# Chunk-wise products of w from a product tree through DRAM, in a fused RWKV-7 and gated-FFN kernel

## The chip, the cores and the metric

The kernel runs on one core of a Trainium2 chip. The number that counts is the device time of one execution in microseconds. The kernel before has a median of 846.03 us over 8 runs (844.63 to 849.34). A single execution was taken apart by the hardware profiler; that one took 847.05 us.

In what follows PE is TensorE's matmul side and PEld its weight load, DVE is VectorE, ACT is ScalarE, POOL is GpSimd and SP is SyncE, which here only issues DMAs.

## The reference

Two blocks, one behind the other. The first is a recurrence over 768 time steps with a 40 x 40 state for each of 4 batches and 8 heads, the second a feed-forward block on 3072 tokens of 320 features:

```python
B, H, S, D = r.shape                      # 4, 8, 768, 40
for t in range(S):
    y[:, :, t] = einsum('bhd,bhde->bhe', r_t, state)
    Sa = einsum('bhde,bhe->bhd', state, a_t)
    state = state * w_t[:, :, None, :] - einsum('bhd,bhe->bhde', Sa, b_t)
    state = state + einsum('bhd,bhe->bhde', v_t, k_t)
x = y.transpose(0, 2, 1, 3).reshape(3072, 320)
h = x @ w_in                              # w_in 320 x 2048, w_out 2048 x 320
out = (h * cos(h)) @ w_out
```

w lies between 0.85 and 0.95. w_in and w_out come as 64-bit floats, which the kernel turns into 32-bit ones in its first part, from the raw words.

## The kernel before

**Chunks.** The recurrence runs in 24 chunks of C = 32 steps. Inside a chunk it is done with matrices, and for that every chunk needs W, the running product of w over its steps: a is multiplied by W one step earlier (`wx`, whose first entry is 1), b and k are divided by W (multiplied by the reciprocal `rw`), and the state is multiplied by W of the last step (`wc`) at the chunk's end. In natural layout a tile has batch and time on the partitions, 4 x 32, and heads and features along the row. Transposed it has two heads' features on the partitions and, per pair of heads, batch and time along the row.

**p1, the first preparation, by pairs of chunks.** `p1_w` (L330) transposes w of two chunks on PE into one PSUM pair (`wT`). ACT copies the first time step into `w1`, DVE clears that step in PSUM, and a `tensor_tensor_scan` per chunk (L340) gives the running products in `wb`. POOL copies the last step out as `wc`. `p1_a` (L345), once for each chunk, transposes `wb` back on PE into `wn`, transposes a beside it, and then DVE takes the reciprocal of `wn` (`rw`, L361) and multiplies a's transpose by `wx` into `aT` (L363); POOL sets the first entry of `wx` to 1 (L357) and makes b times `rw` (`bn`, L366). `p1_b` transposes `bn`, `p1_n` multiplies aT by bT. For each four chunks DVE then inverts 32 x 32 triangular matrices for all of them at once: `inverse`, 31 steps of two instructions (L414, L418) between two transposes (L406, L422), whose result `rt` is needed by `ch_s` of the first of the four.

**p2 and main, by chunk.** `p2_v`, `p2_k` and `p2_g` make the transposes of v, r and k and the Gram matrices; `ch_t`, `ch_q`, `ch_x`, `ch_s` and `ch_z` carry the state `qz` through the chunk and write `yt`, which goes through DRAM (`xd`) and comes back as `xT`.

**The second part.** The feed-forward block is cut into pieces (`first_a`, `first_b` and two `second` for each of 12 groups of tokens and 4 column blocks). Pieces of tokens that are ready fill the gaps of the recurrence; those that are left run at the end, from about 665 us on without any p1.

**The order** is written out by hand. For each chunk the list `segs` names t, v, q, k, x, g, s, z, the p1 segments pw, pa, pa1, pb, pn of a later pair, and M, a place for a piece. The loop issues them in turn; `fill` says how many steps of the inverse and of the weights' conversion go in after each. If the list comes to s while `rt` is missing, pieces are issued, each with four inverse steps, until it is there. `later(n, work)` issues work, mostly DMAs, n steps on. The p1 of a pair lies one to four chunks ahead of its use: pairs 4 and 6 in chunk 3, pair 8 in chunk 4, 10 in 5, 12 in 7, 14 in 9, 16 in 11, 18 in 13, 20 in 15, 22 in 17. Chunk 4 begins at 182 us in the profile, chunk 5 at 228, chunk 7 at 293, chunk 11 at about 418 and chunk 15 at about 542.

**PSUM.** `at` gives PSUM pairs in turn from a ring of two. A new user waits until the last reader of the user before last is through.

**DMA queues.** SP issues nearly all loads in order, four DMAs of 40 KB for each tensor and chunk, in pieces of 160 bytes. At the start ACT issues a of chunks 0 and 1, POOL a of chunks 2 and 3.

**Filler.** `busy` and `shifted` issue matmuls on zeros (`idle`) whose result nobody uses: `shifted` one-column ones, 56 in chunk 2 and 48 in chunk 19.

Of the kernel before, what the change touches and what calls it, by code (L numbers as in the profile page):

```python
# [12 lines left out]
ALU = mybir.AluOpType  # L13
# [7 lines left out]
def kernel(  # L21
# [124 lines left out]
    def load(c, names, via=nc.sync):  # L146
        for n in names:
            for i in range(B):
                via.dma_start(
                    nat[n, c][blk[i], :, :D],  # L150
                    src[n][i, :, c * C : (c + 1) * C, :].rearrange("h t d -> t h d"),
                )

    for c in range(2):
        load(c, "w")
        load(c, "a", nc.scalar)
    for n, c in (("b", 0), ("b", 1), ("w", 2), ("w", 3), ("b", 2), ("b", 3)):
        load(c, n)
    load(0, "kvr")

# [8 lines left out]
    load(2, "a", nc.gpsimd)  # L169
    load(3, "a", nc.gpsimd)  # L170
# [4 lines left out]
    w1 = kept("w1", [P, 4 * B, C], 2, 0.0, on=nc.vector)  # L175
    bn_b = kept("bn", [P, H, DP], 7, 0.0, padding, nc.vector)
    kn_b = kept("kn", [P, H, DP], 2, 0.0, padding, nc.vector)
# [7 lines left out]
    idle = const.tile([P, 512], BF16, tag="idle", name="idle")  # L185
# [144 lines left out]
    def p1_w(c):  # L330
        ps = at("wT")
        for i in range(2):
            turned(ps[:, i], nat["w", c + i])

        for i in range(2):
            nc.scalar.copy(w1[i][:, :, 0:1], b4(ps[:, i])[:, :, 0:1])
        nc.vector.memset(ps[:, :, ::C], 0.0)
        for i in range(2):
            wb = ring.tile([P, 4 * P + 1], F32, tag="wb", name="wb")
            nc.vector.tensor_tensor_scan(wb[:, 1:], ps[:, i], flat(w1[i]), 0.0, ALU.mult, ALU.add)  # L340
            wc = ring.tile([P, 4 * B], F32, tag="wc", name="wc")
            nc.gpsimd.tensor_copy(wc, wb[:, C::C])
            G["wb", c + i], G["wc", c + i] = wb, wc

    def p1_a(c):  # L345
        if c < 4:
            wn = ps_h.tile([P, 512], F32, tag="h", name="wn")
            aps = ps_o.tile([P, 512], F32, tag="o", name="aps")
        else:
            ps = at("wn")  # L350
            wn, aps = ps[:, 0], ps[:, 1]
        for j in range(4):
            nc.tensor.transpose(
                wn[:, j * P : (j + 1) * P], G["wb", c][:, j * P + 1 : (j + 1) * P + 1], ident
            )

        nc.gpsimd.memset(G["wb", c][:, : 4 * P : C], 1.0)  # L357
        G["wx", c] = b4(G["wb", c][:, : 4 * P])
        turned(aps, nat["a", c])
        rw = ring.tile([P, H, D], F32, tag="rw", name="rw")  # L360
        nc.vector.reciprocal(rw, unpad(wn.rearrange("p (h d) -> p h d", h=H)))  # L361
        aT = ring.tile([P, 4, P], F32, tag="aT", name="aT")
        nc.vector.tensor_tensor(  # L363
            aT.rearrange("p j (b t) -> p (j b) t", b=B), b4(aps), G["wx", c], ALU.mult
        )
        nc.gpsimd.tensor_tensor(unpad(bn_b[c % 7]), unpad(nat["b", c]), rw, ALU.mult)  # L366
        G["rw", c], G["aT", c] = rw, aT
# [207 lines left out]
    def ch_z(c):  # L575
# [3 lines left out]
        for bb in range(B):  # L579
            for e in range(2):  # L580
                mm(
                    ps[bb // 2][full[e], bb % 2, : 4 * N72], idle[blk[bb], :DP],
                    idle[blk[bb], : 4 * N72], True,
                )
# [147 lines left out]
    def p1(c):  # L732


        def first_w():
            p1_w(c)
            if c == 4:
                for i in range(2):
                    later(1, lambda i=i: load(6 + i, "w"))

        def an_a(i):
            p1_a(c + i)
            if c == 4:
                later(1, lambda: load(6 + i, "ab"))
            elif i and c >= 2 and c + 3 < NCH:
                for m in range(6):
                    later(
                        9 + m // 3 if c == 2 else 2 + m, lambda m=m: load(c + 2 + m % 2, "wab"[m // 2])
                    )

        return [first_w, lambda: an_a(0), lambda: an_a(1), lambda: p1_b(c), lambda: p1_n(c)]
# [17 lines left out]
    with tc.manual_schedule():  # L769
# [24 lines left out]
        def busy(n, after=False):  # L794


            ps = ps_h.tile([P, 512], F32, tag="h", name="busy")
            if after:
                nc.vector.memset(tick, 1.0)
                nc.tensor.matmul(  # L800
                    ps[:1, :], lhsT=tick, rhs=idle, start=True, stop=True, skip_group_check=True
                )
            for _ in range(n):
                mm(ps, idle[:, :P], idle, True)
# [8 lines left out]

        first, other = p1(0), p1(2)
        for seg in (*first[:3], *other[:3], *first[3:], *other[3:]):
            step(seg)
        p2_in(0)
# [4 lines left out]
        for n, seg in ((12, v), (0, k), (0, g), (6, main(0)[2]), (6, None), (4, v1), (0, k1), (0, g1)):  # L822
            for _ in range(n):
                inv_steps.pop(0)()
            if seg:
                step(seg)
            else:
                for m in range(3):
                    w_work[m][0]()
                p2_in(1)  # L830
                p2_kn(1)
        while inv_steps:
            inv_steps.pop(0)()
            if 2 < len(inv_steps) < 9:
                busy(1, True)
# [16 lines left out]
        N_PAD = {2: 56, 19: 48}  # L852
        M = object()
        for c in range(NCH):
# [10 lines left out]
            elif c == 3:  # L865
                pw4, pa4, pa5, pb4, pn4 = p1(4)
                pw, pa, pa1, pb, pn = p1(6)
                segs = [
                    t, pw4, M, q, pa4, M, x, pa5, M, s, pw, M, pb4, pa, M, pn4, pa1, M, z, M, pb, v,
                    pn, k, M, g,  # L870
                ]
                fill = (2, 3)
            elif c == 4:
                pw, pa, pa1, *p8 = p1(8)
                segs = [t, v, M, q, M, k, x, M, g, M, s, M, z, M, pw, M, pa, pa1, M]
                fill = (2, 0)
            elif c == 5:
                pw, pa, pa1 = p1(10)[:3]
                pb, pn = p8
                segs = [t, M, pb, q, M, pn, v, M, x, k, M, s, pw, M, g, M, z, M, pa, pa1, M]  # L880
            elif c % 4 == 0 and q0 < NCH:
                pb, pn = p1(q0)[3:]
                segs = [t, v, M, q, M, k, x, M, g, M, s, pb, M, z, M, pn, M, M]
            elif c % 4 == 1 and q0 < NCH:
                pw, pa, pa1 = p1(q0 + 2)[:3]
                segs = [t, M, pw, q, M, x, k, M, s, v, M, z, M, pa, M, g, M, pa1, M]
            elif c % 4 == 2 and q0 < NCH:
                pb, pn = p1(q0 + 2)[3:]
                segs = [t, M, pb, q, M, pn, v, M, x, M, s, k, M, g, M, z, M, M]
            elif c % 4 == 3 and q0 + 4 < NCH:  # L890
                fill = (2 if c == 7 else 1, 0)
                pw, pa, pa1 = p1(q0 + 4)[:3]
                segs = [t, M, pw, q, M, x, k, M, s, v, M, z, M, pa, M, g, M, pa1, M]
            else:
                segs = [t, v, M, q, M, x, k, M, g, M, s, M, M, z, M, M]
# [8 lines left out]
            if c in (2, 19):  # L904
# [59 lines left out]
```

## Time and profile before

| | |
|---|---|
| median of 8 runs | 846.03 us (844.63 to 849.34) |
| the profiled execution | 847.05 us, of it 845.0 us span |
| PE busy | 751.0 us, 89% |
| DVE busy | 511.5 us, 61% |
| ACT busy | 377.0 us, 45% |
| POOL busy | 197.2 us, 23% |
| scans of w (L340) | 24, mean 1212 ns |
| reciprocals (L361) | 24, mean 2150 ns |
| transposes wn (L353) | 96, 273 ns median |

The page cuts the span into 40 slices of 21 us and gives each engine's busy share in tenths, and beside it the clock that PE was granted. A view by windows gives busy microseconds in stretches of choice. The list of waits says which engine stood idle until whose instruction ended; the timeline lists instructions with start and duration. PE's matmuls overlap, so the distance between starts says more of their cost than the duration of one.

### The profile page before, as it was taken

How to read it: one execution, taken by the hardware profiler on the slowest of the kernel's cores; microseconds unless marked ns; L12 is line 12 of the kernel's file. 1: busy time of each engine (PE TensorE's matmuls, PEld its weight loads, DVE VectorE, ACT ScalarE, POOL GpSimd, SP SyncE). 2: the span in 40 equal slices, each digit the busy share in tenths (PEclk: the TensorE clock that was granted, in tenths of full speed). 3: DMA queues.
4: the chain of work that ended last, by engine and by line, in shares of the span. 5: the costliest groups of instructions: out<-in, count | busy, mean ns of one | idle time of the engine just before them, and what ended most of it. 6: DMA issues, size and time to landing. Idle time of an engine off the chain costs nothing.

```text
span 845.0 us, 37607 instructions
## 1 busy us (share of the span) xinstructions
PE 751.0 (89%) x16830; PEld 576.5 (68%) x16830; DVE 511.5 (61%) x1076; ACT 377.0 (45%) x707; POOL 197.2 (23%) x343
## 2 busy tenths in 40 slices
PE   4447777996898979999998999998999999999997
PEld 3424456774676757787776777776777777777775
DVE  8688868779534796335796345796355784323331
ACT  1216676353153433546344436435445443554343
POOL 4405634230303203212221221230221222011000
PEclk9758889998899999999998999999999999999999
DMA  7556453331133312313214114224211211101000
GB/s 98 108 86 184 126 149 85 63 68 35 39 54 57 60 36 53 64 36 68 55 37 82 44 26 70 54 40 71 54 26 36 46 33 43 36 20 35 19 16 16
DMA packets 181856, 49.10 MB, mean 58 GB/s; under 512 B 156992, under 2 KB 178496, under 8 KB 181696
## 3 DMA queue, kind: packets, MB, share of 16 engines
q1 hardware_dynamic: 179264, 46.05, 27.0%
q8 instruction: 132, 2.16, 1.0%
q10 hardware_dynamic: 2176, 0.33, 0.3%
q0 software_dynamic: 256, 0.33, 0.2%
q14 instruction: 28, 0.23, 0.1%
HBM read 38.80 MB, written 7.86 MB: 55 GB/s over the span
## 4 chain that ended last, share of the span: by engine, by line
PE 64%; DVE 23%; ACT 7%; issue 3%; DMA 2%; POOL 0%; SPq 0%; ACTq 0%; DVEq 0%
PE ph L101 23%; PE po L101 19%; DVE inv_tmp L414 5%; DVE inv L418 5%; PE dps L101 3%; PE x0ps L101 3%; PE gram L101 2%; PE vT L298 2%; PE sps L101 2%; PE nps L101 2%; DVE rw L361 2%; DVE turns L678 2%; DVE wb L340 1%; PE qps L101 1%; DVE gT L686 1%
## 5 line engine op out<-in xcount | busy, mean ns | idle before, releaser
L101 PE MATMUL po<-w_out_sb,gT 128*128 128x320 f32 x768 | 225.3, 440 | 0.0
L101 PE MATMUL ph<-xT,w_in_sb 128*128 128x256 f32 x768 | 192.2, 397 | 4.9 <-DVE gT L686 3.7
L101 PEld LDWEIGHTS po<-w_out_sb,gT 128*128 128x128 f32 x768 | 140.4, 191 | 53.9 <-issue 2.6
L101 PEld LDWEIGHTS ph<-xT,w_in_sb 128*128 128x128 f32 x768 | 144.6, 197 | 34.2 <-issue 13.4
L676 ACT ACTIVATE turns<-ph,rnd 128x512 f32<-128x512 f32 x96 | 63.8, 686 | 161.7 <-PE ph L101 161.4
L678 DVE SCALAR_TENSOR_TENSOR turns<-turns,ph 128x512 f32<-128x512 f32 x96 | 63.7, 683 | 113.2 <-ACT turns L676 113.1
L603 POOL TENSOR_TENSOR qz<-qz,wc 128x160 f32<-128x160 f32 x92 | 42.7, 482 | 257.2 <-DVE qz L602 256.5
L686 DVE TENSOR_TENSOR gT<-ph,turns 128x512 f32<-128x512 f32 x96 | 65.8, 686 | 36.8 <-ACT turns L683 36.8
L414 DVE TENSOR_TENSOR inv_tmp<-u,inv 128x31 f32<-128x31 f32 (+15 forms) x186 | 71.0, 382 | 4.4
L418 DVE TENSOR_TENSOR inv<-inv,inv_tmp 128x31 f32<-128x31 f32 (+15 forms) x186 | 69.1, 372 | 6.4
L683 ACT ACTIVATE turns<-turns,half_pi 128x512 f32<-128x512 f32 x96 | 69.3, 722 | 3.1
L682 ACT ACTIVATE turns<-turns 128x512 f32<-128x512 f32 x96 | 60.2, 627 | 21.6 <-DVE turns L678 21.6
L361 DVE RECIPROCAL rw<-wn 128x320 f32<-128x320 f32 x24 | 51.6, 2150 | 7.9 <-PE wn L298 7.7
L101 PE MATMUL ph<-xT,w_in_tail 64*128 64x256 f32 x384 | 55.1, 405 | 0.0
L602 DVE TENSOR_TENSOR qz<-dps,qz 128x160 f32<-128x160 f32 x92 | 28.9, 315 | 33.0 <-PE dps L101 32.9
L508 ACT COPY s<-sT 128x512 f32<-128x512 f32 x46 | 24.6, 586 | 51.6 <-PE sT L504 51.6
L101 PEld LDWEIGHTS ph<-xT,w_in_tail 64*128 64x128 f32 x384 | 33.6, 189 | 10.7 <-issue 7.1
L614 POOL TENSOR_TENSOR yt<-yt,wb 128x512 f32<-128x512 f32 x24 | 31.3, 1302 | 22.4 <-DVE yt L609 22.4
L436 POOL COPY vp<-nat_v 128x320 f32<-128x320 f32 x25 | 12.0, 481 | 95.5 <-DMA nat_v<-in_v_dram 66.2
L101 PE MATMUL sps<-x,rt 32*32 32x72 f32 x1536 | 22.6, 242 | 13.1 <-DVE rt L422 10.9
L101 PEld LDWEIGHTS sps<-x,rt 32*32 32x32 f32 x1536 | 18.0, 110 | 22.9 <-issue 16.5
L520 ACT COPY qz<-qps 40x512 f32<-40x512 f32 x46 | 26.6, 579 | 13.4 <-PE qps L101 12.9
(117 smaller groups left out, 1049.7 us busy)
## 6 DMA issues: line engine op xcount, KB each, us to landing
words<-in_moe_w_in_dram SPq DMA_DIRECT2D x8, 512.0 KB
nat_k<-in_k_dram SPq DMA_DIRECT2D x96, 40.0 KB
nat_v<-in_v_dram SPq DMA_DIRECT2D x96, 40.0 KB
nat_r<-in_r_dram SPq DMA_DIRECT2D x96, 40.0 KB
xd<-yt SPq DMA_DIRECT2D x48, 80.0 KB
out_dram<-ot SPq DMA_DIRECT2D x24, 160.0 KB
nat_w<-in_w_dram SPq DMA_DIRECT2D x88, 40.0 KB
nat_b<-in_b_dram SPq DMA_DIRECT2D x88, 40.0 KB
```

Source lines behind the costliest of these rows:

```text
L101: nc.tensor.matmul(o, lhsT=lhsT, rhs=rhs, start=start, stop=stop, skip_group_check=True)
L361: nc.vector.reciprocal(rw, unpad(wn.rearrange("p (h d) -> p h d", h=H)))
L414: nc.vector.tensor_tensor(tmp, u[:, j : j + 1, :j].to_broadcast([P, C - j, j]), x[:, j:, j : j + 1].to_broadcast([P, C - j, j]), ALU.mult,)
L418: nc.vector.tensor_tensor(x[:, j:, :j], x[:, j:, :j], tmp, ALU.subtract)
L602: nc.vector.tensor_tensor(z, pick(dp, 0, (2 * N72 + C, 2), (N72, 2), (1, D)), z, ALU.add)
L603: nc.gpsimd.tensor_tensor(z, z, wc.rearrange("p (f m b) -> p f m b", f=2, m=2)[:, :, :, bb] .unsqueeze(3).to_broadcast([P, 2, 2, D]), ALU. ...
L614: nc.gpsimd.tensor_tensor(yt.rearrange("p j b t -> p (j b) t"), yt.rearrange("p j b t -> p (j b) t"), wx, ALU.mult)
L676: nc.scalar.activation(n, u, ACTF.Identity, bias=rnd, scale=1.0)
L678: nc.vector.scalar_tensor_tensor(n, n, -ROUND, u, ALU.add, ALU.subtract)
L682: nc.scalar.activation(n, n, ACTF.Abs)
L683: nc.scalar.activation(n, n, ACTF.Sin, bias=half_pi, scale=-2.0 * math.pi)
L686: nc.vector.tensor_tensor(gT[:, 2 * e : 2 * e + 2].rearrange("p f t -> p (f t)"), us[e], ns[e], ALU.mult)
```

## The change

From chunk 4 on W is no longer scanned in the transposed layout. For four chunks (a quartet) w is fetched into one tile `ws` with batch, head and chunk on the partitions (4 x 8 x 4 = 128) and the 32 steps along the row; a product tree of nine multiplies on DVE, done in place, turns it into running products; the tile is stored to DRAM (`wd`), and the loads that fetched w fetch W from there. `p1_w` then only transposes it, and ACT copies it to `wb`. The reciprocal reads the loaded tile instead of a PSUM tile, so the transposes back (`wn`) are gone for these 20 chunks. Chunks 0 to 3 keep the scan.

a's transposes of a pair stand in one segment in one PSUM pair, so pa1 is gone from the lists; the first chunk's reciprocal is issued in pw, the second's in pa behind both aT. The trees stand in chunk 3 (for 8 to 11), 4 (12 to 15), 8 and 12; the first one (4 to 7) at the very start, its fetch being the first DMA on ACT's queue and its store on POOL's. In chunk 4 two places for pieces move from behind s to ahead of it. Besides, the memsets of `bn` and `kn` padding move from DVE to POOL, `w1` lives in the ring of `gT`, `idle` is smaller and read with step 0, and the filler is 111 one-column matmuls ahead of the end of the first inverse and 75 in chunk 19, none in chunk 2.

```diff
+                at_c = src[n][i, :, c * C : (c + 1) * C, :]
+                if n == "w" and c >= 4:
+                    at_c = wd[c // 4][i, :, c % 4]
+    ws = const.tile([P, C, D], F32, tag="ws", name="ws")
+    def ws_fetch(q, via=nc.sync):
+        n = 4 * C * D
+        via.dma_start(
+            ws.rearrange("p t d -> p (t d)"),
+            bass.AP(w.tensor, w.offset + q * n, [[S * D, B * H], [C * D, 4], [1, C * D]]),
+        )
+    def ws_scan(q):
+        n = 1
+        while n < C:
+            to = ws[:, 2 * n - 1 :: 2 * n]
+            nc.vector.tensor_tensor(to, to, ws[:, n - 1 :: 2 * n], ALU.mult)
+            n *= 2
+        n = C // 4
+        while n:
+            to = ws[:, 3 * n - 1 :: 2 * n]
+            nc.vector.tensor_tensor(to, to, ws[:, 2 * n - 1 : C - 1 : 2 * n], ALU.mult)
+            n //= 2
+    def ws_store(q, via=nc.sync):
+        wd[q] = dram.tile([B, H, 4, C, D], F32, tag="wd", name="wd")
+        via.dma_start(wd[q].rearrange("b h c t d -> (b h c) (t d)"), ws.rearrange("p t d -> p (t d)"))
+    ws_fetch(1, nc.scalar)
     for c in range(2):
         load(c, "w")
         load(c, "a", nc.scalar)
...
     load(0, "kvr")
+    ws_scan(1)
...
+    ws_store(1, nc.gpsimd)
...
-    bn_b = kept("bn", [P, H, DP], 7, 0.0, padding, nc.vector)
-    kn_b = kept("kn", [P, H, DP], 2, 0.0, padding, nc.vector)
+    bn_b = kept("bn", [P, H, DP], 7, 0.0, padding)
+    kn_b = kept("kn", [P, H, DP], 2, 0.0, padding)
...
             wb = ring.tile([P, 4 * P + 1], F32, tag="wb", name="wb")
-            nc.vector.tensor_tensor_scan(wb[:, 1:], ps[:, i], flat(w1[i]), 0.0, ALU.mult, ALU.add)
+            if c < 4:
+                nc.vector.tensor_tensor_scan(
+                    wb[:, 1:], ps[:, i], flat(G["w1"][:, i]), 0.0, ALU.mult, ALU.add
+                )
+            else:
+                nc.scalar.copy(wb[:, 1:], ps[:, i])
...
+            if c >= 4:
+                from_one(c + i)
+        if c >= 4:
+            over_w(c, unpad(nat["w", c]))
+    def from_one(c):
         nc.gpsimd.memset(G["wb", c][:, : 4 * P : C], 1.0)
+    def over_w(c, wn):
         rw = ring.tile([P, H, D], F32, tag="rw", name="rw")
+        nc.vector.reciprocal(rw, wn)
+        nc.gpsimd.tensor_tensor(unpad(bn_b[c % 7]), unpad(nat["b", c]), rw, ALU.mult)
...
+    def p1_a(c):
+        if c >= 4:
+            ps = at("aps")
+            for i in range(2):
+                turned(ps[:, i], nat["a", c + i])
+            for i in range(2):
+                a_W(c + i, ps[:, i])
+            over_w(c + 1, unpad(nat["w", c + 1]))
+            return
...
+    def scanned(q):
+        ws_scan(q)
+        later(2, lambda: ws_store(q))
+        if q + 1 < NCH // 4:
+            later(12, lambda: ws_fetch(q + 1))
...
-        N_PAD = {2: 56, 19: 48}
+        N_PAD = {0: 111, 19: 75}
+        shifted(N_PAD[0])
...
-                    t, pw4, M, q, pa4, M, x, pa5, M, s, pw, M, pb4, pa, M, pn4, pa1, M, z, M, pb, v,
-                    pn, k, M, g,
+                    t, pw4, M, q, pa4, M, x, lambda: scanned(2), M, s, pw, M, pb4, pa, M, pn4, M, z, M,
+                    pb, v, pn, k, M, g,
...
-                segs = [t, v, M, q, M, k, x, M, g, M, s, M, z, M, pw, M, pa, pa1, M]
+                segs = [t, v, M, q, M, k, x, M, g, M, M, M, s, pw, z, M, pa, lambda: scanned(3), M]
...
-                segs = [t, M, pw, q, M, x, k, M, s, v, M, z, M, pa, M, g, M, pa1, M]
+                segs = [t, M, pw, q, M, x, k, M, s, v, M, z, M, pa, M, g, M, M]
```

Where w of chunks 6 and 7 and their a and b are loaded moves too: w of 6 behind pw of pair 4, w of 7 and then a and b of both behind its pa.

## Prediction

> **What bounds it now.** I read the page's slices first, then busy time by stage, TensorE's waits and the timeline at the worst gap.
>
> ```profile
> PE   4447777996898979999998999998999999999997
> DVE  8688868779534796335796345796355784323331
> PEclk9758889998899999999998999999999999999999
> PE 64%; DVE 23%; ACT 7%; issue 3%; DMA 2%; POOL 0%; SPq 0%; ACTq 0%; DVEq 0%
> ```
>
> PE is full from slice 9 on, with a dip every fourth chunk (about 124 us), where DVE stands at 9. The stages, in us (columns: PE, PEld, DVE, ACT, POOL busy; clock; DMA share):
>
> ```profile
> 183.00:213.00 30.00, 20.26 (x450) 15.81 (x450) 26.54 (x67) 12.08 (x22) 1.26 (x2) 0.88 0.22 40
> 292.00:332.00 40.00, 32.67 (x662) 25.34 (x661) 35.80 (x76) 13.85 (x27) 9.58 (x18) 1.00 0.20 40
> 332.00:416.00 84.00, 83.97 (x2136) 65.90 (x2135) 37.77 (x84) 42.65 (x82) 15.40 (x31) 1.00 0.31 58
> 416.00:455.00 39.00, 34.84 (x671) 27.53 (x670) 37.01 (x79) 14.02 (x27) 12.28 (x21) 0.95 0.28 54
> 540.00:580.00 40.00, 35.84 (x674) 28.23 (x673) 38.01 (x80) 15.10 (x29) 12.29 (x21) 0.97 0.29 54
> 580.00:665.00 85.00, 85.00 (x2135) 66.40 (x2135) 40.72 (x88) 41.43 (x79) 16.86 (x32) 0.99 0.19 39
> ```
>
> Two regimes: PE sets the time at 332 to 416 and from 580 on, DVE at under half; in chunks 3-4, 7, 11 and 15 an inverse and the W of the next quartet keep DVE 89 to 95% busy and PE waits. What PE waits for after 150 us:
>
> ```profile
> PE sps L101 <- DVE rt L422: 9.3, 1, 9.3
> PE vT L298 <- DVE aT L363: 8.0, 3, 3.8
> PE sT L504 <- DVE aT L363: 3.8, 2, 2.0
> PE sps L101 <- DVE x L546: 2.2, 1, 2.2
> PE x0ps L101 <- DVE wb L340: 1.8, 1, 1.8
> ```
>
> So 11.8 us wait for aT (13.1 with 1.3 of wT<-aT). Chunk 11 shows why:
>
> ```profile
> 445.30 0.60 PE L353 MATMUL wn<-ident,wb 128*128 128x128 f32 x4
> 445.74 0.60 PE L298 MATMUL wn<-ident,nat_a 128*128 128x128 f32 x4
> 446.18 2.32 PE L101 MATMUL po<-w_out_sb,gT 128*128 128x320 f32 x8
> 450.33 2.15 DVE L361 RECIPROCAL rw<-wn 128x320 f32<-128x320 f32 x1
> 452.40 0.63 DVE L363 TENSOR_TENSOR aT<-wn,wb 128x512 f32<-128x512 f32 x1
> 453.17 1.09 PE L298 MATMUL vT<-ident,vp 128*128 128x128 f32 x4 [3.78 <-DVE aT L363]
> ```
>
> The PSUM pair that vT wants is held by wn/aps until aT has read it, and aT queues behind a 2.15 us reciprocal. The clock is 0.66 in 450 to 460, so vT then takes 1.09 instead of about 0.65.
>
> **The change by parts.**
>
> *Removed on PE.* Four wn transposes for each of 20 chunks. A row says 273 ns each, but the starts above lie 0.44 us apart per four: 0.11 each. 80 x 0.11 = 8.8 us, or 0.88 per pair of chunks. Here a rule differs: the Trainium skill, "TensorE: Matmul & The Clock Gate", Part 4, gives about 275 ns per transpose in a kernel's context, and says that the full clock doesn't engage for transposes. By it 80 are worth 22 us. The 273 ns is latency; successors start after 110, so I take 8.8.
>
> *Removed and added on DVE.* 20 scans of 1.21 and ten memsets of 0.085: 25.1 us; in chunk 11 the stretch is 0.4 (waiting for ACT's copy) + 0.1 + 2.34 for the pair = 2.8 per dip. The 24 reciprocals stay (2.15). Added: five trees of nine multiplies on 640, 320, 160, 80, 40, 40, 120, 280, 600 = 2,280 elements. Inverse rows give 0.20 us at 31 elements and 0.43 at 255: about 0.17 + 1.0 ns per element; with 0.03 between ops a tree is 2.28 + 1.53 + 0.27 = 4.1 us. Four fall inside, 16.4: DVE gains 8.7 in all, but the scans go from the dips, while the trees lie in chunks 3, 4, 8, 12. In the last two PE is the bound and DVE under half, so cost 0; without that cover, 4.1 each. Chunk 3 has none: two pairs of scans (4.9) against one tree, -0.8.
>
> A rule against the trees: "SBUF — State Buffer", SBUF: two separate sides, says DVE with two SBUF inputs and a GpSimd op reading SBUF lock each other out. The trace agrees: inv_tmp on 207 elements takes 1.35 at 540.96 beside POOL's yt (1.27), against a median of 0.37. The scan, with one PSUM input, wasn't exposed. By the inverse's rows a tree costs 4.1; by the rule, beside one yt, 5.4, which would put 5.2 on the sum if the four weren't covered. I keep 4.1, since PE covers them.
>
> *Reordered.* a's transposes no longer wait for wb, and both aT (2 x 0.63) come ahead of the pair's second reciprocal; the first, reading SBUF, moves into the pw segment, in the scan's place (2.15 for 2.34). The aT waits should go: 3.8 each in chunks 11 and 15, 1.8 in 4, 2.0 in 5, 1.3 in 3. What is late next: in 5, ph waits for xT's DMA until 263.2 anyway, so I count 0.6 there; in 11 and 15 vvm L493, done at 448.2, five us before aT.
>
> *ACT.* Two wb copies per pair, about 0.59 (row of bT), less two of 0.19: +8 us over the run, at 45% busy. Covered; uncovered, 0.8 per pair.
>
> *POOL.* wc and the wb memset now follow ACT. bn moves to the w segment and waits there for the reciprocal; behind it queue kn, vvm, vp and z's qz. POOL idles 10.95 ahead of qz in chunk 11: 0; if not covered, 2.15 per pair. The padding memsets go from DVE (9 x 0.22) to POOL (some 0.3 each, after ident's 0.20), behind a2/a3's issues (4.78) and the store of W, which waits for the first tree; they delay wc and bn of chunk 0 by 0 to 1.
>
> *SP and DMA.* Each quartet adds a 655 KB fetch and store and makes w's loads wait for the store. SP takes about 0.5 us per issue and waited 241 us for yt in all, DMA is 20 to 30% busy: 0 inside, except the third rival. Chunk 4's pass queues 16 loads (a, b of 6 and 7) at once, some 8 us of SP time ahead of k/v/r and xd; w7 goes first, and the same loads were there in two lots: 0, to +2.
>
> *Start.* No row shows a fetch beside the first loads. From below, 0 (hidden). From above, both w loads wait for all of it: 655 KB at 328 to 410 GB/s (the rate while words load) is 1.6 to 2.0, more when the tree (4.1) and w1's memset (1.0) run over w's arrival: 6. The first tree is a new DVE wait, for the fetch; queued behind it are w1's memset and the first scan, on which PE's wn waits. Fetch landing at some 6, tree to 10.2, memset to 11.2, w transposed at 12.2 (10.2 before): covered by 1 us. POOL's new wait for that tree also holds half_pi, so ACT's warm-up (1.28 + 0.2) comes later, behind the first w copies as now. I take +2, because from 11 to 62 us the chain runs through DVE to the inverse.
>
> *Filler.* 111 one-column matmuls where PE idles 6.6 us (51 to 58): 2.9 at 26 ns (48 in 1.27), or double when cold; 0. Chunk 2's 56 go where PE isn't the bound: 0, to -1.5. Chunk 19: 27 more, +0.7. The smaller idle tile, read with step 0, streams as many columns: 0.
>
> *Chunk 4.* Before, the loop already ran two to three pieces at s while rt was missing, and the trace has six before sps at 212.3. Two more places issue inverse steps that those forced pieces issued, so I count one more, not two: one po x8, 3.54 cold at 213.5, moved into the 9.3 us gap. I take -2.5 (0 to -6).
>
> **Sum against 847.05** (that execution; span 845.0, 2.05 around it), in us:
> - start +2
> - chunk 3: PE -1.8, waits (wn<-wb 3.9, wT<-aT 1.3) half replaced by other DVE work, DVE's balance 0: in all -3
> - chunk 4, ahead of s -2.5; its p1(8): -0.9 - 1.8, with 0.2 lost to the next wait: -2.5
> - chunk 5: -0.9 - 0.6 = -1.5
> - chunk 7: no aT wait, but x0ps<-wb 1.8, x 2.2, dps 1.5: relief 2.8 on DVE and PE's 0.9 partly hidden: -3.5
> - chunks 9, 13, 17: -0.88 each: -2.6
> - chunk 11: 3.8 + 0.9 + cold clock (1 - 0.66) x 6.8 = 2.3: 7.0, I take -6; chunk 15: 3.8 + 0.9 + 1.3 = 6.0, I take -5.5
> - chunk 19 +0.7
>
> Total -24.4: 822.7, and against the median shown (846.03, 1.02 lower) 821.6; I say 822.
>
> **Rivals.**
> 1. *DVE keeps the bound* (0.20): in the dips another DVE result (x, vvm, rt) is late as soon as aT isn't. Against: aT is five us behind vvm; for: DVE is 95% busy. Then 2.8 in each of 7, 11, 15, 8.8 x 0.7 of PE and 1.5 in chunk 4, less 2: 847 - 14 = 832 on the median.
> 2. *The start is exposed* (0.11): +6 instead of +2, and the rest as forecast: 826.
> 3. *SP is held* (0.05), the slower one: in-order SP stands at a store until DVE has finished the tree, or at w's loads until it has landed; xd, xT and k/v/r queue behind, ph starves and the clock falls. The four SP stores must cost over 24.4/4 = 6.1 us each to cancel the gain; at 8.5 each: 846 - 24.4 + 34 = 856. For: xT already ends one wait (1.2). Against: two steps between tree and store, nothing of DVE late in chunks 8 and 12.
> 4. *It isn't what it says* (0.02): more pieces ahead of s is one, and TensorE's "issue" stalls move with instruction counts: 846.
>
> Forecast 0.62. Range: all waits, cold clock and start at their good ends give about -35 (811); rival 1 with the exposed start gives 836, rounded to 837. Rival 3 and the rest stay outside. A measurement of this kernel tells about 0.2% from no change. Faster by more: 0.62 + 0.20 + 0.11 = 0.93, less 0.01 for rival 1's tail: 0.92; within 0.02; slower 0.06.
>
> **What would show it.** wn falls from 96 transposes to 16, scans from 24 to 4; vT<-aT gone from PE's waits; chunks 11 and 15 at clock 1.0 with DVE below 90%; trees near 4.1 us; the first sps some 2 us after 61.7; PE's gap before chunk 4's sps under 7. Wrong if vT waits for another DVE tile, SP waits for DVE at a store, or the inverse starts much later than 31.2.

## The result, and the profile after

| | before | after |
|---|---|---|
| median (32 runs before, 11 after) | 846.8 us (844.09 to 849.34) | 839.41 us (836.84 to 841.88) |
| ratio, 95% interval | | 0.9916, 0.9903 to 0.9928 |
| span of the profiled execution | 845.0 us | 837.9 us |
| DVE, ACT busy | 511.5, 377.0 us | 505.5, 383.9 us |

The change wins 7 us where 24 were forecast, so the time lies above the range.

Some names for what follows: ph and po are the first and the last product of a second-part piece, turns the step on DVE behind ph, sps the product of segment s, which needs the inverse `rt`; the tokens of a chunk are its `yt`, stored as xd and read back as xT. SPq is SP's queue. The slices and the chain of the page after:

```profile
PE   3547678877688988999999999999999999999997
...
DVE  7788787864855498264599454796353774323231
...
PEclk9857798997899998999999999999999999999999
...
PE 64%; DVE 18%; ACT 5%; DMA 5%; issue 3%; POOL 2%; SPq 2%; DVEq 0%; ACTq 0%; POOLq 0%
```

The dips of PE in slices 22 and 28 (the ends of chunks 11 and 15 and the starts of 12 and 16) are filled, 8 to 9. New is what stands near slice 10: DVE falls from 9 to 4, the clock from 8 to 7, and the chain has 5% DMA and 2% SP, where it had 2% and none. PE's waits from 120 us on (us in total, times, longest) name it:

```profile
PE ph L101 <- DMA xT<-xd: 12.4, 2, 8.5
PE sps L101 <- DVE rt L476: 6.5, 1, 6.5
PE sps L101 <- DVE x L600: 4.3, 2, 4.1
...
PE vT L328 <- DVE vvm L547: 1.5, 3, 0.5
```

No wait for aT is left, as forecast. But ph now waits 12.4 us for xT, 8.5 of them at the start of chunk 4 and 3.9 in chunk 6; before it was 1.2, in chunk 6.

The first sT of each chunk (the transpose of the state, the first work of its segment t) gives the balance by chunk. Each row is the growth of "after less before" across the stretch:

| stretch | forecast | measured |
|---|---|---|
| start, to the first sps | +2 | +3.4 |
| chunks 1 and 2 | 0 | -0.1 |
| chunk 3 | -3 | -3.5 |
| chunk 4 | -5.0 | **+6.0** |
| chunk 5 | -1.5 | -1.5 |
| chunk 6 | 0 | **+2.8** |
| chunk 7 | -3.5 | **-0.8** |
| chunks 8 to 10 | -0.9 | -1.5 |
| chunks 11 and 12 | -6 | -6.4 |
| chunks 13 and 14 | -0.9 | -0.1 |
| chunks 15 and 16 | -5.5 | -5.8 |
| from 17 on | -0.2 | +0.4 |
| sum | -24.5 | -7.1 |

Of the 17.4 us missing, chunk 4 has 11.0, chunk 6 2.8, chunk 7 2.7 and the start 1.4; the other rows give 0.5 back.

**Chunk 4.** SP's queue after, in the timeline (start, duration, and how many DMAs of that kind):

```profile
147.26 9.62 SPq L152 DMA_DIRECT2D nat_w<-wd  x8
156.99 1.88 SPq L152 DMA_DIRECT2D nat_a<-in_a_dram  x4
...
174.99 5.15 SPq L152 DMA_DIRECT2D nat_w<-wd  x8
180.24 4.74 SPq L152 DMA_DIRECT2D nat_a<-in_a_dram  x8
185.02 0.59 SPq L161 DMA_DIRECT2D ws<-in_w_dram  x1
185.71 2.01 SPq L152 DMA_DIRECT2D nat_b<-in_b_dram  x4
187.82 0.74 SPq L677 DMA_DIRECT2D xd<-yt  x2
...
191.20 0.39 SPq L687 DMA_DIRECT2D xT<-xd  x1
```

POOL finished yt of chunk 3 at 176.04. Before the change SP was through its loads by then and waited for yt:

```profile
176.34 0.69 SPq L623 DMA_DIRECT2D xd<-yt  x2
...
184.88 1.89 PE L101 MATMUL ph<-xT,w_in_sb 128*128 128x256 f32 x8
...
212.29 1.25 PE L101 MATMUL sps<-x,rt 32*32 32x72 f32 x64 [9.28 <-DVE rt L422]
```

Now xd goes out at 187.82, because SP issues in order, a tensor's four DMAs take it 1.9 us, and it is behind: w and a of chunks 8 and 9, a fetch and b of 8 stand ahead of xd, and b of 9 between xd and xT. On PE after the change:

```profile
193.30 3.78 PE L101 MATMUL ph<-xT,w_in_sb 128*128 128x256 f32 x8 [8.50 <-DMA xT<-xd]
...
222.76 1.25 PE L101 MATMUL sps<-x,rt 32*32 32x72 f32 x64 [6.48 <-DVE rt L476]
```

ph then takes 3.78 instead of 1.89, as the clock has fallen (granted 0.50 over 193.3 to 197.1). DVE works at turns<-ph next in its order, so the inverse stands behind it too: the first sps, which waits for rt, comes at 222.76 where it came at 212.29.

### The profile page after: what moved, and what is told of

Same layout as the page of the kernel before. It is cut to its first block, busy times and chain, and to the rows that moved or that the text cites. A ratio compares the mean times of both kernels' runs of the same rounds, so it can differ in the third digit from the quotient of the medians.

```text
span 837.9 us, 37660 instructions
## 1 busy us (share of the span) xinstructions
PE 744.9 (89%) x16832; PEld 571.0 (68%) x16832; DVE 505.5 (60%) x1081; ACT 383.9 (46%) x707; POOL 199.9 (24%) x353
## 3 DMA queue, kind: packets, MB, share of 16 engines
q8 instruction: 132, 2.16, 1.1%
## 4 chain that ended last, share of the span: by engine, by line
PE 64%; DVE 18%; ACT 5%; DMA 5%; issue 3%; POOL 2%; SPq 2%; DVEq 0%; ACTq 0%; POOLq 0%
PE ph L101 23%; PE po L101 19%; DVE inv L472 4%; DVE inv_tmp L468 4%; PE dps L101 3%; PE x0ps L101 3%; PE gram L101 3%; PE vT L328 2%; PE sps L101 2%; DVE rw L391 2%; PE nps L101 2%; PE qps L101 2%; PE sT L558 1%; DVE turns L732 1%; DMA xT<-xd 1%
## 5 line engine op out<-in xcount | busy, mean ns | idle before, releaser
L101 PE MATMUL ph<-xT,w_in_sb 128*128 128x256 f32 x768 | 191.0, 395 | 16.2 <-DMA xT<-xd 12.4
L472 DVE TENSOR_TENSOR inv<-inv,inv_tmp 128x31 f32<-128x31 f32 (+15 forms) x186 | 71.5, 385 | 6.4
L468 DVE TENSOR_TENSOR inv_tmp<-u,inv 128x31 f32<-128x31 f32 (+15 forms) x186 | 68.8, 370 | 4.5
L562 ACT COPY s<-sT 128x512 f32<-128x512 f32 x46 | 24.5, 584 | 45.6 <-PE sT L558 45.6
L391 DVE RECIPROCAL rw<-nat_w 128x320 f32<-128x320 f32 x20 | 42.8, 2142 | 0.0
L574 ACT COPY qz<-qps 40x512 f32<-40x512 f32 x46 | 26.6, 579 | 17.4 <-PE qps L101 17.0
```

The costliest lines, as they stand in the source:

```text
L101: nc.tensor.matmul(o, lhsT=lhsT, rhs=rhs, start=start, stop=stop, skip_group_check=True)
L391: nc.vector.reciprocal(rw, wn)
L468: nc.vector.tensor_tensor(tmp, u[:, j : j + 1, :j].to_broadcast([P, C - j, j]), x[:, j:, j : j + 1].to_broadcast([P, C - j, j]), ALU.mult,)
L472: nc.vector.tensor_tensor(x[:, j:, :j], x[:, j:, :j], tmp, ALU.subtract)
```

## The experiments

My theory after the result: chunk 4 is lost on SP, where the tokens of chunk 3 stand behind loads; the start is lost to DMA time; chunk 7 never had a relief; chunks 11 and 15 were won by aT coming earlier. The rivals: that the moved places hold up chunk 4, that the tree costs the start, that the tree wins the dips. Ratios are to the kernel before, which was run again beside each set of kernels (medians 846.5 to 847.6); the changed kernel's is 0.9916. What an edit is worth "on the median" is taken from the ratios, 0.001 being 0.85 us; lengths of chunks and waits are those of the one profiled execution.

### What chunk 4 waits for

**tokens_ahead**

```diff
-    8 + m // 3 if c == 2 else 2 + m            # steps until a load is issued
+    8 + m // 3 if c == 2 else 6 + m if c == 6 and m > 1 else 2 + m
```

> The changed kernel, but a's and b's loads of chunks 8 and 9 are issued four steps later, so that chunk 3's xd and xT come ahead of them on SP. Theory (tokens of chunk 3 stand behind loads on the in-order SP): ph's wait for xT at 184.8 falls from 8.5 us to under 3, the first sps of chunk 4 goes from 222.8 to about 214, and the time from 839.4 to 830 (828 to 834). Rival (the three places ahead of s, or the transfers themselves, cost chunk 4): the wait or the first sps stays, 837 to 841.

Measured: 834.37 us, 0.9848 (0.9819 to 0.9876), just above the 828 to 834 that the theory expected. SP's and PE's lines:

```profile
178.34 0.87 SPq L677 DMA_DIRECT2D xd<-yt  x2
183.43 0.39 SPq L687 DMA_DIRECT2D xT<-xd  x1
...
185.07 5.34 SPq L152 DMA_DIRECT2D nat_a<-in_a_dram  x8
...
185.59 1.99 PE L101 MATMUL ph<-xT,w_in_sb 128*128 128x256 f32 x8 [1.01 <-DMA xT<-xd]
```

xd is 9.5 us earlier, the wait 1.0 instead of 8.5, and chunk 4 takes 43.0 us (51.3 after, 45.3 before). With nothing changed but the order of loads on SP, the theory holds. The first sps comes at 212.78. On the median 5.8 of those 8.2 us remain.

**w67_late**

```diff
-    later(1, lambda: load(6, "w"))          # behind pw4
...
-    later(1, lambda: load(7, "w"))          # behind pa4, ahead of a, b of 6 and 7
-    for i in range(2):
-        later(1, lambda i=i: load(6 + i, "ab"))
+    for n, i in (("a", 6), ("a", 7), ("b", 6), ("w", 6), ("w", 7), ("b", 7)):
+        later(1, lambda n=n, i=i: load(i, n))
```

> The changed kernel with the loads of W of chunks 6 and 7 issued behind a of 6 and 7 and b of 6. Theory (SP stood 8.3 us at these two loads for the reciprocals, which now read nat_w itself, and that is over half of xd's delay of 11.4 us): SP no longer stands at 147 to 157, chunk 3's xd goes out at 180 to 184 instead of 187.8, the wait for xT falls from 8.5 to 1 to 5, time 831 to 836. Rival (only the number of loads queued ahead of xd counts): xd within 2 us of 187.8, 838 to 840.

Measured: 835.51 us, 0.9864 (0.9844 to 0.9884).

```profile
148.06 3.79 SPq L152 DMA_DIRECT2D nat_a<-in_a_dram  x8
151.94 1.88 SPq L152 DMA_DIRECT2D nat_b<-in_b_dram  x4
153.91 5.13 SPq L152 DMA_DIRECT2D nat_w<-wd  x8
...
181.02 0.73 SPq L677 DMA_DIRECT2D xd<-yt  x2
```

The eight w DMAs take 5.1 instead of 9.6 us, xd is 6.8 us earlier, the wait for xT falls to 0.8, and chunk 4 takes 41.3 us. Part of that gain is lost in chunk 3, where PE now waits 1.7 us for the later W; that chunk takes 2.9 us more. So the delay has two causes: SP stood at these loads for the reciprocals (8.3 us of "SPq <- DVE rw" in the waits of the changed kernel), since these now read `nat_w`, which the load overwrites, and no longer PSUM; and the counted loads came earlier relative to the tokens, since a pair has a segment less. Either one taken away is enough.

**places_back** and **tok_places**, with and without the SP delay:

```diff
-    segs = [..., x, M, g, M, M, M, s, pw, z, M, pa, ...]
+    segs = [..., x, M, g, M, s, M, z, M, pw, M, pa, ...]
```

> The changed kernel with chunk 4's two places back behind s, z and pw as before. Theory (SP is the cause): the 8.5 us wait for xT stays, the gap before sps grows by one piece of 2.4 to 3.6, the time is 840 to 842. Rival (the two places hold s back and cause chunk 4's loss): 830 to 834.

> tokens_ahead with chunk 4's two places back behind s, pw behind z. Theory (places_back lost 5.5 mainly because W of pair 8 came later, so that bn and bT held nps and a cold clock doubled the pieces behind; that doesn't depend on the tokens): 838 to 841, ratio 0.990 to 0.993. Rival (the two places are worth one piece of 2.4 to 3.5, as the prediction took them): 836.5 to 838.

Measured: 845.38 us, 0.9980 (0.9966 to 0.9995), slower than either expectation of places_back, and 839.11 us, 0.9901 (0.9870 to 0.9932), as the theory of tok_places had it. So the edit is worth 5.4 and 4.5 us. The rival, that the places do harm, falls. Of 5.1 us in tok_places' record 1.9 are chunk 4's (rt is waited for 8.5 us instead of 6.6), about the forecast's piece of 2.5; 3.2 are chunk 5's. places_back shows how:

```profile
244.41 1.32 PE L101 MATMUL nps<-aT,bT 40*32 40x32 f32 x128 [2.16 <-ACT bT L429]
246.75 1.12 PE L328 MATMUL vT<-ident,vp 128*128 128x128 f32 x4 [1.03 <-ACT qz L574]
247.66 1.06 PE L328 MATMUL vT<-ident,rp 128*128 128x128 f32 x4
248.51 4.23 PE L101 MATMUL po<-w_out_sb,gT 128*128 128x320 f32 x8
```

With pw behind z, bn and bT of pair 8 are late; PE waits 0.7 for bn and 2.2 for bT, the clock falls (granted 0.55 over 248.5 to 252.8), and po takes 4.23 instead of 2.32.

### The start

**start_late**, **start2**

```diff
-    ws_fetch(1, nc.scalar)      # ahead of all loads
...
+    ws_fetch(1)                 # behind b of 0 to 3, on SP
...
-    ws_scan(1)
-    ws_store(1, nc.gpsimd)
...
+        ws_scan(1)              # behind the fourth aT
+        later(2, lambda: ws_store(1))   # start_late: on SP
+        ws_store(1, nc.gpsimd)          # start2: on POOL, behind kn of chunk 0
...
-    8 + m // 3 if c == 2        # start2 only
+    8 + m // 3 * 2 if c == 2
```

> The changed kernel with the first fetch of W behind b's loads on SP and its tree after the fourth aT, where DVE waits 5.2 us for nt. Theory (the fetch takes DMA time from the first w loads, and all of that is on the path to the first inverse): the second wT goes from 12.5 back to about 9.1, the first sps of chunk 0 earlier by 3, time 836 to 837. Rival (it is taken back by a later wait, the tree in its new place or PE's queue): within 1 of 839.4.

> start_late, but the first store of W goes to POOL behind chunk 0's kn, and three of the six loads that follow chunk 2's a are issued two steps later, so that k, v and r of chunk 2 come ahead of them on SP. Theory (in start_late the 3.2 us won at the first sps were lost to v and r of chunk 2, which stand behind those loads on SP and hold POOL's qz): PE's 5.3 us wait for POOL's qz at 68 to 73.4 goes, the first sT comes at about 70.3 (73.8 in the changed kernel), time 835 to 837. Rival (something else of the start takes it back): the first sT comes after 73 again, 839.

Measured: 839.76 us, 0.9905 (0.9879 to 0.9932), and 836.95 us, 0.9884 (0.9863 to 0.9906). First PE of the kernel before, then SP and PE of the changed kernel and of start2:

```profile
9.10 1.09 PE L298 MATMUL wT<-ident,nat_w 128*128 128x128 f32 x4 [2.69 <-DMA nat_w<-in_w_dram]
```

```profile
0.82 7.13 SPq L152 DMA_DIRECT2D nat_w<-in_w_dram  x8
...
12.54 1.09 PE L328 MATMUL wT<-ident,nat_w 128*128 128x128 f32 x4 [3.70 <-DMA nat_b<-in_b_dram]
```

```profile
0.82 4.86 SPq L152 DMA_DIRECT2D nat_w<-in_w_dram  x8
...
9.31 1.09 PE L326 MATMUL wT<-ident,nat_w 128*128 128x128 f32 x4 [2.74 <-DMA nat_w<-in_w_dram]
```

With the fetch behind, the eight w loads leave SP 2.3 us sooner and the second wT begins 3.2 us earlier, close to where it began before the change (9.10). (The row of the changed kernel names nat_b, but this transpose reads nat_w; releasers are inferred.) The first tree had ended at 10.7 in the changed kernel, ahead of that wT: the fetch's DMA time was the cost, not the tree. start_late reached sps at 61.95 (65.12 after) and lost all of it 11 us on:

```profile
73.43 0.69 PE L556 MATMUL sT<-ident,qz 128*128 128x128 f32 x2 [5.30 <-POOL qz L655]
```

POOL stood 25.5 us for v of chunk 2, which SP had queued behind w, a and b of 4 and 5. With that order mended, in start2, the first sT comes at 70.05 (73.8 after), and 2.7 us stay on the median. It is chunk 4's story once more: load order on SP was the next limit.

### What won chunks 11 and 15

**recip_ahead**

```diff
+            over_w(c + 1, unpad(nat["w", c + 1]))
             for i in range(2):
                 a_W(c + i, ps[:, i])
-            over_w(c + 1, unpad(nat["w", c + 1]))
```

> The changed kernel with the second reciprocal of each pair put ahead of the two aT again. Theory (the 5.7 and 5.9 us won in chunks 11 and 15 come from aT ahead of the reciprocal): vT or sT waits for aT again, 1 to 2 us in chunks 4, 5, 7 and 3 to 6 in 11 and 15, and the time rises by 6 to 12 to 845 to 851. Rival (they come from the scans that left the dips): rises by 0 to 2.

Measured: 838.23 us, 0.9893 (0.9872 to 0.9913): no slower, where the theory expected 6 to 12 us more, and no wait for aT. In chunk 11 both aT still end at 449.6, 3.4 us ahead of vvm's product on DVE. The order against the reciprocal is worth nothing; my theory in this form falls, and so does the prediction's.

**two_segs**, **two_segs2**

```diff
+            if c > 4:                # in p1_a
+                turned(ps[:, 0], nat["a", c])
+                a_W(c, ps[:, 0])
+                return
...
+    def p1_a1(c):
+        ps = at("aps")
+        turned(ps[:, 0], nat["a", c + 1])
+        over_w(c + 1, unpad(nat["w", c + 1]))
+        a_W(c + 1, ps[:, 0])
...
-    segs = [..., z, M, pa, M, g, M, M]
+    segs = [..., z, M, pa, M, g, M, pa1, M]
```

> tokens_ahead with a's transposes of a pair in two segments again from chunk 6 on, the second one behind g and its reciprocal ahead of aT, as before the change; W still by the tree. Theory (what chunks 11 and 15 won is that the pair's second aT comes two segments earlier, whichever side of the reciprocal it is on): vT or sT waits for aT again, 2 to 4 us in each of 11 and 15, and the time is 7 to 12 above that of tokens_ahead: ratio 0.993 to 0.999. Rival (they were won by the wn transposes and scans that are gone): ratio 0.985 to 0.988.

> two_segs with the loads of the next pairs counted from the second segment, so that no load comes ahead of a reader (in two_segs w of the next pair overwrote the second chunk's W ahead of its reciprocal, which then waited for that load: bn was late in chunks 10 and 14 and its W a wrong one). Theory (chunks 11 and 15 were won by the second aT being two segments earlier): vT waits for aT 2 to 4 us in 11 and 15 again, and the time is 5 to 10 above tokens_ahead: 840 to 845, ratio 0.991 to 0.997. Rival (they were won by the wn transposes and scans that are gone): no wait for aT, 834 to 837, 0.985 to 0.988.

two_segs took 847.27 us, 0.9997. In it the next pair's W is loaded over the second chunk's W before the reciprocal has read it, so that it computes with a wrong W, waits for that load, and tells nothing of aT. In two_segs2 the loads of the next pair are counted from the second segment: 842.08 us, 0.9925 (0.9897 to 0.9954), 6.5 us above tokens_ahead. First PE of the changed kernel at the start of chunk 12, then DVE and PE of two_segs2:

```profile
453.83 0.63 PE L328 MATMUL vT<-ident,vp 128*128 128x128 f32 x4 [0.53 <-DVE vvm L547]
```

```profile
452.46 2.14 DVE L391 RECIPROCAL rw<-nat_w 128x320 f32<-128x320 f32 x1
454.52 0.63 DVE L397 TENSOR_TENSOR aT<-aps,wb 128x512 f32<-128x512 f32 x1
...
455.30 0.63 PE L328 MATMUL vT<-ident,vp 128*128 128x128 f32 x4 [2.38 <-DVE aT L397]
```

The wait of before is back (2.4 in chunk 12, 2.7 in 16), so the second aT two segments earlier does free PSUM in time. But the time of two_segs2 as a whole meets its expectation by luck. Against the changed kernel chunks 11 and 12 together lose 1.7 us and 15 and 16 together 3.8, which is less than half of the 12.1 won there. More, 8.4 us against tokens_ahead, goes in chunk 4: the new count of the loads puts the tokens of chunk 3 behind a wait once more (xT is issued at 188.00 instead of 183.43).

```profile
190.26 3.78 PE L101 MATMUL ph<-xT,w_in_sb 128*128 128x256 f32 x8 [6.82 <-DMA xT<-xd]
```

**scan_merged**, **scan_merged2**: tokens_ahead with W by the scan throughout, wn transposed ahead of a in the merged segment; in scan_merged2 also the filler of before.

```diff
-            if c < 4:                # in p1_w
+            if True:
...
-            ps = at("aps")           # in p1_a
+            wn, ps = at("wn"), at("aps")
...
-        N_PAD = {0: 111, 19: 75}     # scan_merged2 only
+        N_PAD = {2: 56, 19: 48}
```

> tokens_ahead with W of every chunk by the scan, as before the change, its wn transposes ahead of a's in the merged segment; no tree, no fetch and no store of W. Theory (the merge alone wins chunks 11 and 15, and the tree brings 0.9 per pair and costs 3.4 at the start): 11 and 15 stay without a wait for aT, the start is 3.4 earlier, eight to ten pairs cost 0.9 each and DVE's scans some 2 in chunk 7: 832 to 838, ratio 0.984 to 0.990. Rival (the tree is what wins the dips): 841 to 846, 0.994 to 0.999.

> scan_merged with the filler of the kernel before (56 one-column matmuls in chunk 2, 48 in chunk 19, none in chunk 0). Theory (scan_merged stood 26.7 us in 22 stalls of PE marked issue, against 4.0 in 4 of the kernel before, only because the number of PE's instructions no longer fitted the filler; the merge itself wins the dips without the tree): the stalls fall under 10 us, 838 to 846, ratio 0.990 to 0.999. Rival (the stalls come from wn's transposes standing in front of a's in one segment): 860 or more.

Measured: 867.69 us, 1.0246 (1.0202 to 1.0291), and 846.6 us, 0.9988 (0.9978 to 0.9997). The first one fits neither theory: PE stood 26.7 us in 22 waits marked "issue", for which the profile shows no releaser, most of them in the middle of a group of matmuls. With the old filler count 6.7 in 4 are left, and the kernel is 22 us faster. In its record chunks 11 and 12 together take 4.1 us less than before, 15 and 16 together 3.2 less, where the changed kernel wins 6.4 and 5.8. So the merge alone brings somewhat over half of the dips' gain. The rest goes with the scans and wn transposes. But the same kernel takes 6.9 us more than before in chunk 3. A wait of 1.7 for ACT's qz is in it, and an issue wait with a cold clock behind it (granted 0.82 over 172 to 191):

```profile
173.59 2.08 PE L101 MATMUL ph<-xT,w_in_tail 64*128 64x256 f32 x8 [2.66 <-issue]
175.60 3.78 PE L101 MATMUL ph<-xT,w_in_sb 128*128 128x256 f32 x8
```

Before, these groups took 1.13 and 1.89, so this one wait costs 5.5 us. As it stands, the merge without the tree gains nothing on the whole.

### The filler

**pads_before**

```diff
-        N_PAD = {0: 111, 19: 75}
-        shifted(N_PAD[0])
+        N_PAD = {2: 56, 19: 48}
...
-            if c == 19:
+            if c in (2, 19):
                 shifted(N_PAD[c])
```

> The changed kernel with the filler of the kernel before: 56 matmuls in chunk 2 and 48 in chunk 19 in place of 111 in chunk 0 and 75 in chunk 19. Theory (the filler's count sets where PE's instruction stream stalls, so it is worth more than the time it runs): PE's issue stalls rise from 5.8 to 15 to 30 us and the time to 850 to 865. Rival (it is time filled and no more, as the prediction took it): 838 to 840.

Measured: 851.84 us, 1.0051 (1.0038 to 1.0065), 11.4 us above the changed kernel, from 82 one-column matmuls fewer and their place. From 62 us on, PE's issue waits rise from 5.8 us in 7 to 13.2 in 14. One of them, in the timeline of PE in chunk 21:

```profile
730.79 0.29 PE L101 MATMUL gram<-rT,vT 40*32 40x32 f32 x13 [1.37 <-issue]
731.01 1.80 PE L101 MATMUL ph<-xT,w_in_tail 64*128 64x256 f32 x8
732.74 2.97 PE L101 MATMUL ph<-xT,w_in_sb 128*128 128x256 f32 x8
```

Behind the wait of 1.37 the granted clock is 0.60 over 731 to 732.7 and 0.66 over 732.7 to 735.7: the next two groups take 1.80 and 2.97 where they take 1.13 and 1.99 at full clock, so that it costs 3.0 in all. That is how 7.4 us more of waits can make the 12.8 by which the two profiled executions differ.

### Chunks 6 and 7, and all of it together

**tok_recip**

```diff
-        if c >= 4:                            # in p1_w
+        if c == 4 or c % 4 == 2 and c > 4 or c == 8:
             over_w(c, unpad(nat["w", c]))
...
+            if c % 4 == 0 and c > 8:          # in p1_a, behind both aT
+                over_w(c, unpad(nat["w", c]))
```

> tokens_ahead with both reciprocals of the pairs 12, 16 and 20 behind the two aT, none in the segment of w. Theory (chunk 7 kept its length because a reciprocal of 2.15 stands in the inverse where the two scans of 2.34 stood, and DVE bounds that chunk): PE's wait for x in chunk 7 falls from 4.1 to about 2, and chunk 7 is 1.5 to 2.5 shorter; ratio 0.982. Rival (the reciprocal only moves to where it holds up something else in the same stretch): 0.985 or above.

Measured: 835.13 us, 0.9874 (0.9839 to 0.9909), which on the median is no gain over tokens_ahead. By chunks both hold: chunk 7 takes 33.5 us instead of 36.1 and the wait for x falls from 4.1 to 1.6, but chunk 12 takes 1.7 and chunk 16 3.3 us more. There DVE is the bound again:

```profile
435.92 4.15 DVE L391 RECIPROCAL rw<-nat_w 128x320 f32<-128x320 f32 x2
...
443.75 0.42 DVE L549 TENSOR_TENSOR vvm<-gram,su 128x256 f32<-128x256 f32 x1 [0.44 <-ACT vvm L548]
...
444.32 0.63 PE L328 MATMUL vT<-ident,vp 128*128 128x128 f32 x4 [2.30 <-DVE vvm L549]
```

**pair_swap**

```diff
+        firsts = [...]                        # first_a and first_b of this piece
+        seconds = [...]                       # the two second of the piece before
...
+        pieces.extend(seconds + firsts if (g, j) == (2, 0) else firsts + seconds)
```

> tokens_ahead with the two last second-part pieces of the token pair of chunks 2 and 3 put ahead of the first first-part piece of chunks 4 and 5, so that the first piece of chunk 6 needs no xT. Theory (what chunk 5 won was lost at ph's wait of 3.9 us for xT in chunk 6, since xT lands 9.8 us after chunk 5's dps in both kernels): the wait goes, chunk 6 is 2.5 to 4 us shorter, 830 to 832. Rival (another wait, rt of chunk 8 or DVE's inverse in 6 and 7, takes it back): 834.

Measured: 831.5 us, 0.9806 (0.9771 to 0.9840), 3.6 us below tokens_ahead. ph no longer waits in chunk 6 for xT, chunk 6 takes 32.8 us instead of 34.9; a new wait for gT of 2.3 us takes part of the 3.9. (The profiled execution is the slowest of its six; an issue wait of 1.5 makes its chunk 5 longer.)

**best1** (start2, w67_late and tok_recip in one), **best2** (with pair_swap), **best3** (best1, but the reciprocal moved for pair 12 alone), **best4** (best3 with pair_swap):

```diff
-        if c >= 4:                            # best3, best4
+        if c >= 4 and c != 12:
             over_w(c, unpad(nat["w", c]))
...
+            if c == 12:                       # in p1_a, behind both aT
+                over_w(c, unpad(nat["w", c]))
```

> start2, w67_late and tok_recip in one kernel. Theory (start 3.4, SP's two causes and chunk 7's reciprocal are separate): from 834.4 of tokens_ahead, 2.5 to 3.5 at the start and 1 to 3 in chunk 7: 828 to 831, ratio 0.977 to 0.981. Rival (the start's gain is lost at chunk 4's inverse or at the next load on SP, as in start_late): 832 to 835.

> best1 with pair_swap's order of pieces. Theory (separate waits): 830.3 less 2 to 3.5, 827 to 828.5, ratio 0.975 to 0.977. Rival (rt of chunk 8 is the next wait): 830.

> best1 with the first reciprocal moved behind the two aT only for pair 12 (chunk 7); pairs 16 and 20 have it in the segment of w as in the changed kernel. Theory (in tok_recip chunk 7 won 2.5 us, while in chunks 11 and 15 the two reciprocals in a row made vvm late, 2.3 us of wait each and a cold clock behind it, about 1.7 and 3.3 us lost): 830.3 less 4 to 6.5, 824 to 826, ratio 0.972 to 0.975. Rival (the losses in 12 and 16 have another cause): 829 to 831.

> best3 with pair_swap's order. Theory (best2 found no gain on the median from the swap because rt of chunk 8 is the next limit, though its record is 1 us shorter): within 1.5 of best3. Rival (the gain of 2.9 that pair_swap showed on tokens_ahead adds): 821 to 823.

| kernel | median us | ratio (interval) |
|---|---|---|
| best1 | 830.28 | 0.9791 (0.9763 to 0.9820) |
| best2 | 832.78 | 0.9810 (0.9790 to 0.9830) |
| best3 | 828.09 | 0.9787 (0.9765 to 0.9809) |
| best4 | 824.71 | 0.9749 (0.9726 to 0.9772) |

best1 meets its expectation; best2 adds nothing that can be told; best3 reaches neither of its two. Its chunks 12 and 16 are 2.9 and 3.6 us shorter than best1's, so the two reciprocals in a row had cost that. But the record of best3 has chunk 5 at 35.5 us instead of 31.9, and the median moved little. In that chunk:

```profile
251.68 0.49 PE L101 MATMUL dps<-vvm,kn 32*40 32x72 f32 x32 [1.69 <-issue]
251.96 0.94 PE L101 MATMUL dps<-sm,bn 32*40 32x72 f32 x64
252.84 4.07 PE L101 MATMUL po<-w_out_sb,gT 128*128 128x320 f32 x8
```

An issue wait of 1.69 and a po that took 4.07 instead of 2.42 account for 3.3 of the 3.6. best4, with another order of pieces and issue waits of 5.2 us in all (10.1 in best3), is between its two expectations, and at 824.71 us the fastest of all, 2.5% under the kernel before.

## Why the prediction was wrong

- **SP and DMA "0 inside", chunk 4's 16 loads "0, to +2".** This is the step that failed. It cost 8.5 us of wait and a cold clock: of the 11.0 us missing in chunk 4, tokens_ahead gives 8.2 back, and best1, with both causes out, 10.1. I had counted the same loads in another grouping, and overlooked two things the diff shows: the reciprocal's source moved from PSUM to `nat_w`, so that a load must wait for DVE; and with a segment less per pair every counted load moves against the tokens. The third rival had the right queue and the right consequence (xT late, ph starved, a cold clock), but priced it at the four stores: SP waited for DVE at none of them, and each took it 0.4 us. The loads took the rest, once, in chunk 4.
- **Chunk 4, "ahead of s -2.5".** Mis-sized: 4.5 to 5.4 us. One piece more was right (1.9 in the record); that pw ahead of z makes bn and bT timely was not seen.
- **Chunk 7, -3.5.** Its relief of 2.8 on DVE contradicts the same text's own line that a reciprocal of 2.15 takes the place of 2.34 of scans. From the same turns<-ph to the copy of x DVE took 20.4 us before and 20.5 after; one step of the inverse behind the reciprocal took 0.96 there instead of 0.42. tok_recip shows that the reciprocal's place is worth 2.5 there: rival 1 is true in chunk 7, and in 11 and 15 DVE is a reciprocal away from it.
- **Chunk 5, -1.5.** Right up to the first sT of chunk 6, and then lost: xT lands 9.8 us after the first dps of chunk 5 (10.1 before), whatever PE does meanwhile, and so chunk 6 lost 2.8. The text named that wait for the aT term and not for the 0.9 of the transposes.
- **Start, +2.** Measured 3.4, near the middle between its bounds 0 and 6. The tree, its new wait and POOL's were covered as worked out; DMA time alone was mis-sized: the second wT begins 3.4 us later, where 1.6 to 2.0 was worked out for the fetch.
- **Chunks 11 and 15, -11.5.** Right in size (-12.2 with the chunks behind), but in part by luck, as the reason was wrong: aT's place against the reciprocal is worth nothing. Its place two segments earlier is worth about half, 5.5 us by what two_segs2 loses and 7.3 by what scan_merged2 wins. The other half went with the scans and the wn transposes; no run here parts these two.
- **Transposes, tree, scans.** wn fell from 96 to 16 and scans from 24 to 4. Inside the recurrence three trees took 3.9 us, near the 4.1 worked out, and one 4.4, in which a multiply beside POOL's bn took 1.02 instead of 0.49. Chunk 9 won 0.9, as worked out; chunk 13 won nothing, for it had two short issue waits and took 1.0 us more than in tokens_ahead.
- **Filler "0".** Wrong as a reading, harmless in the sum: with the filler of before the changed kernel would have been 11.4 us slower. That its waits move with instruction counts stood in the fourth rival.

The forecast's 822 was not reached by any kernel here. best4, with the causes named above taken out and with another order of pieces, which the forecast did not have, needs 824.71.

## What to carry to other kernels

Whenever an edit changes what an instruction reads, ask which load overwrites that source, and who stands behind this load on its queue. When work is issued by counted steps, write the new order of each DMA queue out before costing it at nothing: here one tensor's four DMAs are 1.9 us of SP, and a row of them ahead of the tokens starved PE. And a hidden 2 us term does not add to a neighbour's if both end at the same late transfer.

## What the hardware showed that I had not expected

PE's waits marked "issue" move with the number of instructions ahead of them: 5.8 us in 7 with the filler of the change, 13.2 in 14 with that of before in the same kernel, 26.7 in 22 with 80 transposes more and the filler unchanged, 6.7 in 4 with the old filler again. The page of the changed kernel has 132 instruction transfers of together 2.16 MB, 16.4 KB each. The Trainium skill, "Runtime: NRT & Kernel Launch", Instruction fetch mechanics, says that the stream comes in blocks of 16 KiB and that crossing a boundary is mostly hidden.

The size agrees, and so does the place. The trace of the changed kernel has 33,970 records of PE's matmuls, weight loads and semaphores, 257 for each transfer. If they are numbered from 0 in order of start, 20 of the 22 waits in scan_merged and 11 of the 14 in pads_before stand at number 193 or 194 behind a multiple of 256. Over all 20 traces, from 62 us on, 99 of 154 do, with 104 of 162 us, and 82 of these 99 are in gram, sps or dps, the groups of small matmuls. Where the 256 records ahead had all begun within 3.5 us, 65 of 135 such places have a wait; where that took longer, 34 of 2,369. So a crossing is not always hidden in this kernel: it shows mostly where PE has run through the block ahead quickly, and the filler shifts which work stands there. Between kernels 11 and 22 us hung on it. The other 55 waits stand ahead of kT in chunks 1 and 2 and ahead of aps in chunk 7, whatever the count; their cause stays open.
